# First weights' upper copies and lower parts a tile ahead of use, the first block dealt out anew, U laid out three times

## The chip, the core and the metric

One core of a Trainium2 chip runs the whole program in one launch. The metric is device time in microseconds from start to end of an execution. Engines are named as in the profile: PE (matmul), PEld (its weight loads), DVE, ACT, POOL, and SP, whose queue issues the DMAs.

## The reference

Batch 8, 8 heads, 576 positions, 64 per head, so x is 8 blocks of 576 x 512. All in fp32.

```python
ret = (scale * q @ k.T * Dmat) @ v             # retention, Dmat lower triangular
x   = ret laid out as (B, S, 512)
h   = x.transpose(0, 2, 1) @ U @ V             # U 576 x 32, V 32 x 576: rank 32 over positions
u   = x + h.transpose(0, 2, 1)
x   = u + np.maximum(u @ w_ch1, 0) @ w_ch2     # 512 -> 2048 -> 512
k   = np.maximum(xk @ w_k, 0); v = (k * k) @ w_v
out = sigmoid(xr @ w_r) * v                    # xk, xr: mixes of x and x shifted by one
```

The weights, U and V come in as 64-bit floats, and the kernel makes fp32 of them on the chip.

## The kernel before, in words

An fp32 product is made of three fp32r products: each operand is split into an upper copy (a cast to fp32r by ACT) and a lower part (what the cast left, by DVE or POOL), and upper x upper, lower x upper, upper x lower are summed in PSUM.

The first phase is what the change touches. `seq` runs over 8 batches of 5 chunk pairs (step i is batch i // 5, pair i % 5). A step computes, on PE, `inter(i)` (L842), `own(i)` (L864), `scores(i + 1)` (L808) and `gain(i + 1)` (L886); on DVE `decay`, `from_state`, `states` and `leave`, which end in the tile xt. A step later `natural` transposes xt (PE L950, copied by ACT L960 to xs), two steps later `low_rank` multiplies by U (PE L971, tile gall). When a batch's five are through, its low-rank sum is split (gt), and eight `mix` (PE L1009, DVE L1013) multiply by V and add into xt, which gives u.

Between these the hidden layer of the block of 512 columns before runs: 16 products h (PE L356, `hidden_part`, three parts of four matmuls each), each left by ACT as hs (L362) and stored to DRAM (L367). `FIRST` gives how many h go into each step of the first eight, `FULL` those of the later ones. Half of a step's h come before `stages(2 * i)`, half before `stages(2 * i + 1)`.

The weight w_ch1 is used first by these h. It is cut in four groups of 512 columns (w_0 to w_3; h f uses group f // 4), and each group in four tiles: column half c (h f uses c = (f % 4) // 2), row half j. A tile goes through stages: `load` (SP, L113), `down` (two ACT passes, ca at L97 and cf at L101), `fill` (DVE join L104), and `split` (ACT upper copy w_h L153, DVE lower part w_l L154). The table of `place(...)` says after which half step each stage is written into the program; all engines then run their queues in the written order. `fetch_in_turn` lets only `AHEAD[0]` bytes of loads be under way at once.

Batch 0 is `first_batch()`: no hidden work is there yet, the loads have just begun, and each step runs through its chain alone. `WARM` matmuls on zeros stand ahead of it. After its low-rank sum (`first_sum`) and mixes, h 0 and h 1 are taken together. From step 5 on `step_of(i)` does the above.

Of the kernel before, what the change touches and what calls it, by code (L numbers as in the profile page):

```python
# [9 lines left out]
F32 = mybir.dt.float32  # L10
# [23 lines left out]
WARM = 12  # L34
# [6 lines left out]
def retention_mixer_kernel(ctx: ExitStack, tc: tile.TileContext, io):  # L41
# [67 lines left out]
    AHEAD = [3 << 19]  # L109
# [21 lines left out]
    def convert(fetch, parts, p, n, after=None, eng=nc.gpsimd, halves=False, own=False):  # L131
# [16 lines left out]

        def split():
            h, l = parts()  # L150
            f = got["f"].rearrange("p (k n) -> p k n", n=256) if halves else got["f"]
# [587 lines left out]
    with ExitStack() as st:  # L739
# [223 lines left out]
        gall = []  # L963

        def low_rank(b, p):
            n = CH[p][1]
            if not gall:
                gall.append(bank("g", "gall"))
            x = xn.pop((b, p))
            for k in range(KD):  # L970
                nc.tensor.matmul(  # L971
                    gall[0][32 * k:32 * k + 32, 128 * (b % 4):128 * (b % 4) + 128],
                    ust[:n, p * RANK:(p + 1) * RANK],
                    x[:n, k * 128:(k + 1) * 128],
                    start=(p == 0 and b % 4 == 0),
                    stop=(p == NC - 1),
                    skip_group_check=True,
                )
# [3 lines left out]
        def first_sum(k):  # L982
            if not k:
                gst[0] = a2.tile([96, DM], F32R, tag="gt", name="gt0")
            o, g = slice(k * 128, (k + 1) * 128), gall[0][32 * k:32 * k + 32, 0:128]
            hi, lo, again = (gst[0][r:r + 32, o] for r in (0, 32, 64))
            nc.scalar.copy(hi, g)
            nc.vector.tensor_tensor(lo, g, hi.bitcast(F32), op=ALU.subtract)
            nc.gpsimd.tensor_copy(again, hi.bitcast(F32))

        def low_rank_sum(b):
            gs = small(F32, "gs")[:32]
            gt = a2.tile([96, DM], F32R, tag="gt", name=f"gt{b}")
            for k in range(KD):
                nc.scalar.copy(
                    gs[:, k * 128:(k + 1) * 128],
                    gall[0][32 * k:32 * k + 32, 128 * (b % 4):128 * (b % 4) + 128],
# [52 lines left out]

        def prep_u():
            def fetch():
                raw = big.tile([128, NC * RANK], I64, tag="unit", name="uraw")
# [3 lines left out]
            waiting.append(convert(fetch, lambda: (ust, None), 128, NC * RANK))  # L1057
# [59 lines left out]
        place("u", 1, 2)  # L1117
# [5 lines left out]
        for at in (  # L1123
# [38 lines left out]
        AHEAD[0] = 1 << 20  # L1162
# [3 lines left out]
        load_to(NC + 2)  # L1166
        AHEAD[0] = 0

        def first_batch():
# [6 lines left out]
            for i in range(NC):  # L1176
# [16 lines left out]
                leave(i)  # L1193
                if i:
                    natural(0, i - 1)
                stages(i)
# [6 lines left out]
                if i == 3:  # L1203
                    stages("j0")
# [30 lines left out]
            gain(NC)  # L1235
            decay(NC)
            states(NC)
            ready.extend((0, f) for f in range(2, NF))
# [3 lines left out]
            stages("c1")  # L1242
# [11 lines left out]
        FIRST, FULL = (2, 1, 2, 2, 2, 2, 2, 1), (3, 3, 4, 4, 2)  # L1254
# [349 lines left out]
def _factors(u, v):  # L1604
    u = np.concatenate([u, np.zeros((NC * C - S, RANK), u.dtype)]).reshape(NC, C, RANK)
    return {
        "moe_U": u.transpose(1, 0, 2).reshape(C, NC * RANK),
# [27 lines left out]
```

## Time and profile before

| | us |
|---|---|
| median of 3 runs | 1389.57 (1386.78 to 1391.11) |
| the profiled execution, its own time | 1388.58 |
| its span, first to last instruction | 1386.8 |
| PE busy in the span | 1344.8 (97%) |
| PE's share of the chain that ended last | 89% |
| ACT, DVE, POOL busy | 653.4, 847.7, 338.9 |
| DMA, mean over the span | 222 GB/s |

The page cuts the span into 40 equal slices of 34.7 us and gives the busy share of each engine in each; the phase that the change touches is the first four or five slices. Views of the trace then give busy time by stretch, the waits by who ended them, and the instructions in order of time.

### The profile page before, as it was taken

The page shows a single profiled execution, that of the slowest core. Times are in us where ns is not written, and L with a number is a line of the kernel's source. Part 1 is how long each engine was busy: PE and PEld are TensorE (multiplying, and loading weights), DVE is VectorE, ACT ScalarE, POOL GpSimd, SP SyncE. Part 2 cuts the span into 40 slices and gives each one's busy share as a digit, 9 for nine tenths or more (in the row PEclk, how much of TensorE's full clock was granted, in tenths as well). Part 3 has the DMA queues.
Part 4 walks back from the last instruction along what each step waited for, and adds up shares of the span by engine and source line. Part 5 has one row for each costly group of instructions (what it writes and reads, how often), then busy time and mean ns, then how long its engine had stood idle before and what let it go on. Part 6 is the DMA issues. An engine that isn't in the chain of part 4 may idle for free.

```text
span 1386.8 us, 25835 instructions
## 1 busy us (share of the span) xinstructions
PE 1344.8 (97%) x10296; PEld 1101.0 (79%) x10296; DVE 847.7 (61%) x1175; ACT 653.4 (47%) x1135; POOL 338.9 (24%) x287
## 2 busy tenths in 40 slices
PE   6778899999999999999999999999999999999998
PEld 4556688888888788888887888888888888888897
DVE  3544342333323212689889898698687787787753
ACT  4443344443433455644454444465565455465431
POOL 1111133242131134222122222203303303303312
PEclk8899999999999999999999999999999999999999
DMA  7773669877664465978879696788066075074272
GB/s 247 242 264 123 218 222 322 307 263 256 241 239 156 164 216 201 306 263 280 282 233 334 217 308 217 277 280 318 0 249 237 1 282 203 30 275 151 79 300 77
DMA packets 124377, 307.93 MB, mean 222 GB/s; under 512 B 14496, under 2 KB 27168, under 8 KB 124256
## 3 DMA queue, kind: packets, MB, share of 16 engines
q1 hardware_dynamic: 124256, 306.28, 63.7%
q8 instruction: 81, 1.33, 0.4%
q14 instruction: 40, 0.33, 0.1%
HBM read 215.00 MB, written 91.23 MB: 221 GB/s over the span
## 4 chain that ended last, share of the span: by engine, by line
PE 89%; DVE 2%; ACT 1%; issue 1%; DMA 0%; SPq 0%; DVEq 0%; ACTq 0%
PE h L356 27%; PE v L1471 14%; PE gc L528 6%; PE ga L528 6%; PE gd L528 6%; PE kd L1375 4%; PE kc L1375 4%; PE ka L1375 4%; PE gb L528 3%; PE kb L1375 2%; PE rd L1375 2%; PE rc L1375 2%; PE ra L1375 2%; PE xn L950 1%; PE up L842 1%; PE c L610 1%
## 5 line engine op out<-in xcount | busy, mean ns | idle before, releaser
L362 ACT ACTIVATE hs<-h 128x512 f32<-128x512 f32 x144 | 86.0, 598 | 230.3 <-PE h L356 222.5
L1427 POOL TENSOR_TENSOR vl<-m,vh 128x512 fp32r<-128x512 f32 (+1 forms) x40 | 47.6, 1192 | 310.2 <-ACT vh L1426 240.2
L822 DVE TENSOR_TENSOR pm<-up,dtab 128x512 f32<-128x512 f32 (+1 forms) x40 | 25.5, 637 | 157.2 <-PE up L808 146.3
L487 ACT CAST sbh<-rb 128x1024 fp32r<-128x1024 f32 x64 | 67.3, 1052 | 58.0 <-PE gd L528 47.1
L488 DVE TENSOR_TENSOR sbl<-rb,sbh 128x1024 fp32r<-128x1024 f32 x64 | 85.3, 1333 | 7.9 <-ACT sbh L487 7.7
L1471 PE MATMUL v<-vh,wv_0u 128*128 128x512 f32 x288 | 88.7, 389 | 0.0
L1471 PE MATMUL v<-vh,wv_1u 128*128 128x512 f32 x288 | 88.7, 389 | 0.0
L770 POOL TENSOR_TENSOR kv<-kv,ktab 128x512 f32<-128x512 f32 (+1 forms) x40 | 39.8, 994 | 170.5 <-DMA kv<-in_kv 119.9
L488 DVE TENSOR_TENSOR sal<-ra,sah 128x1024 fp32r<-128x1024 f32 (+1 forms) x64 | 65.5, 1023 | 21.0 <-PE gd L528 13.1
L487 ACT CAST sah<-ra 128x1024 fp32r<-128x1024 f32 (+1 forms) x64 | 53.6, 837 | 50.7 <-DVE ra L469 24.4
L1427 POOL TENSOR_TENSOR vl<-c,vh 128x512 fp32r<-128x512 f32 (+1 forms) x40 | 62.2, 1574 | 25.9 <-ACT vh L1426 25.9
L1471 PEld LDWEIGHTS v<-vh,wv_1u 128*128 128x128 f32 x288 | 54.1, 188 | 11.2
L1471 PEld LDWEIGHTS v<-vh,wv_0u 128*128 128x128 f32 x288 | 53.9, 188 | 11.0
L1426 ACT CAST vh<-m 128x512 fp32r<-128x512 f32 (+1 forms) x40 | 23.2, 579 | 75.3 <-DVE m L1425 75.3
L1013 DVE TENSOR_TENSOR xt<-mx,xt 128x256 f32<-128x256 f32 x64 | 28.9, 457 | 48.6 <-PE mx L1009 48.3
L1471 PE MATMUL v<-vl,wv_0u 128*128 128x512 f32 x144 | 56.0, 389 | 0.0
L1471 PE MATMUL v<-vl,wv_1u 128*128 128x512 f32 x144 | 56.0, 389 | 0.0
L641 ACT ACTIVATE tp<-x2l,omu 128x511 f32<-128x511 f32 x72 | 51.0, 714 | 3.5 <-issue 2.7
L572 POOL TENSOR_TENSOR x<-x,ur 128x512 f32<-128x512 f32 x16 | 24.9, 1572 | 107.7 <-DVE x L568 76.8
L356 PE MATMUL h<-uh,w_0h 128*128 128x512 f32 x144 | 42.9, 421 | 4.0 <-ACT w_0h L153 3.2
L1425 DVE SCALAR_TENSOR_TENSOR m<-m 128x512 f32<-128x512 f32 (+1 forms) x40 | 44.8, 1120 | 1.4
L356 PE MATMUL h<-uh,w_3h 128*128 128x512 f32 x144 | 40.8, 403 | 5.0 <-ACT w_3h L153 5.0
(288 smaller groups left out, 3731.6 us busy)
## 6 DMA issues: line engine op xcount, KB each, us to landing
wk<-keys SPq DMA_DIRECT2D x80, 512.0 KB, 5.9
hp<-hs SPq DMA_DIRECT2D x128, 256.0 KB, 2.7
rb<-hp SPq DMA_DIRECT2D x64, 512.0 KB, 5.9
wr<-gates SPq DMA_DIRECT2D x40, 512.0 KB, 7.4
qk<-in_qk SPq DMA_DIRECT2D x32, 512.0 KB, 5.4
kv<-in_kv SPq DMA_DIRECT2D x32, 512.0 KB, 6.1
ra<-hp SPq DMA_DIRECT2D x32, 512.0 KB, 7.0
ur<-ub SPq DMA_DIRECT2D x18, 512.0 KB, 5.7
```

The source lines that it names most:

```text
L356: nc.tensor.matmul(hps[t, f], w.part(lo, k, fo), u[k // 2][:, k % 2, :], start=(part == 0 and k == 0), stop=(part == 2 and k == KD - 1),)
L362: nc.scalar.activation(h, hps.pop((t, f)), AF.Relu)
L487: nc.scalar.copy(hi_, src)
L488: nc.vector.tensor_tensor(lo_, src, hi_.bitcast(F32), op=ALU.subtract)
L528: nc.tensor.matmul(group[g][p], l[:, col(p)], r, start=(h == 0 and j == 0 and i == 0), stop=(i == 2 and last), skip_group_check=True,)
L641: nc.scalar.activation(tp[:, 1:], x[:, :BT - 1], AF.Copy, scale=omu[:, j, k:k + 1])
L770: nc.gpsimd.tensor_tensor(k, k, ktab[:, p, :n].to_broadcast([128, n, NP, D]), op=ALU.mult)
L1013: nc.vector.tensor_tensor(u, ps[:, :n], u, op=ALU.add)
L1375: nc.tensor.matmul(ps[b], l, r[:, i], start=(part == 0 and i == 0 and j == 0), stop=(i == 1 and j == 2), skip_group_check=True,)
L1425: nc.vector.scalar_tensor_tensor(x, x, 0.0, x, op0=ALU.max, op1=ALU.mult)
L1427: eng.tensor_tensor(l, x, h.bitcast(F32), op=ALU.subtract)
L1471: nc.tensor.matmul(vacc[t][o], w.part(lo, g, col(o)), x[:, i, :], start=(g == 0 and i == 0 and j == 0), stop=(g == NG - 1 and i == 1 and j ...
```

## The change

It does these things, all in the first phase:

- `split` is parted into `upper` (ACT) and `lower` (DVE), each with a place of its own, and the table of places is written anew: a tile's join and upper copy are written one or more half steps ahead of the h that first uses it, and two more tiles (w_1's second column half) are loaded ahead of the hidden work, with a further pair of qk and kv.
- `FIRST` goes from (2, 1, 2, 2, 2, 2, 2, 1) to (2, 1, 2, 1, 1, 2, 2, 3).
- U comes in three times side by side (480 in place of 160 columns). In batch 0 one matmul a chunk, with 96 columns of U stationary and 512 columns of x moving, gives the sum on three groups of 32 partitions; a copy on POOL (`keep`) makes the old `ust` for the later batches. The join of U stands in step 1 in place of step 2.
- The first low-rank sum is split in two halves of 256 columns (one ACT cast of 96 partitions and one DVE subtraction each) in place of four quarters with three instructions each.
- `WARM` is 9 in place of 12, and the loads may be 2 MB ahead at the start (1.5 before) and 1.5 MB at the weights (1 before).

```diff
-WARM = 12
+WARM = 9
-    AHEAD = [3 << 19]
+    AHEAD = [1 << 21]
...
+        def upper():
+            h, l = parts()
+            nc.scalar.copy(h, got["f"].rearrange("p (k n) -> p k n", n=256))
+
+        def lower():
+            h, l = parts()
+            f = got["f"].rearrange("p (k n) -> p k n", n=256)
+            eng.tensor_tensor(l, f, h.bitcast(F32), op=ALU.subtract)
+
+        if halves:
+            return [load, down, fill, upper, lower]
...
         def low_rank(b, p):
-            n = CH[p][1]
-            if not gall:
-                gall.append(bank("g", "gall"))
+            n, c = CH[p][1], p * RANK
             x = xn.pop((b, p))
+            if b == 0:
+                if not p:
+                    gall[0] = bank("g", "g0")
+                nc.tensor.matmul(
+                    gall[0][:96], u_all["x"][:n, 3 * c:3 * c + 96], x[:n], start=(p == 0), stop=(p == NC - 1)
+                )
+                return
...
-        def first_sum(k):
-            if not k:
+        def first_sum(j):
+            if not j:
                 gst[0] = a2.tile([96, DM], F32R, tag="gt", name="gt0")
-            o, g = slice(k * 128, (k + 1) * 128), gall[0][32 * k:32 * k + 32, 0:128]
-            hi, lo, again = (gst[0][r:r + 32, o] for r in (0, 32, 64))
-            nc.scalar.copy(hi, g)
-            nc.vector.tensor_tensor(lo, g, hi.bitcast(F32), op=ALU.subtract)
-            nc.gpsimd.tensor_copy(again, hi.bitcast(F32))
+            gt, g = (x[:96, j * 256:j * 256 + 256] for x in (gst[0], gall[0]))
+            nc.scalar.copy(gt, g)
+            nc.vector.tensor_tensor(gt[32:64], g[32:64], gt[32:64].bitcast(F32), op=ALU.subtract)
...
-            ("w0", "j0", "w joins", "h"), ("w0", "j1", "w joins", "h"), ("w0", "c1", "c1", "c1"), ("w0", "c1", "c1", "c1"),
-            ("w1", 10, 10, 11), ("w1", 10, 11, 11), (10, 12, 13, 14), (10, 13, 14, 14),
-            (11, 14, 15, 16), (11, 15, 16, 16), (13, 16, 17, 18), (13, 17, 18, 18),
-            (15, 18, 19, 20), (15, 19, 20, 20), (17, 20, 21, 22), (17, 21, 22, 22),
+            ("w0", 3, "w joins", "h", "l"), ("w0", "j1", "w joins", "h", "l"),
+            ("w0", "c1", "c1 joins", "c1 h", "c1 h"), ("w0", "c1", "c1 joins", "c1 h", "c1 h"),
+            ("w1", "e", 10, 10, 10), ("w1", "e", 10, 10, 11), ("w2", 11, 12, 13, 13), ("w2", 12, 12, 13, 13),
+            (10, 13, 14, 15, 15), (10, 14, 15, 16, 16), (12, 15, 16, 17, 17), (12, 16, 17, 18, 18),
+            (14, 17, 18, 19, 19), (14, 18, 19, 20, 20), (16, 19, 20, 21, 21), (16, 20, 21, 22, 22),
...
-        AHEAD[0] = 1 << 20
+        AHEAD[0] = 3 << 19
         stages("w0")
         load_to(NC + 1)
         stages("w1")
         load_to(NC + 2)
+        stages("w2")
+        load_to(NC + 3)
         AHEAD[0] = 0
...
             first_sum(0)
+            first_sum(1)
+            stages("h")
             for k in range(KD):
-                if k + 1 < KD:
-                    first_sum(k + 1)
-                if k == KD - 1:
-                    stages("h")
                 for x in range(2):
                     mix(0, k, x)
                 if k % 2:
                     nc.scalar.copy(uh[k // 2], u[:, k - 1:k + 1, :BT])
+            stages("l")
+            stages("c1")
...
-        FIRST, FULL = (2, 1, 2, 2, 2, 2, 2, 1), (3, 3, 4, 4, 2)
+        FIRST, FULL = (2, 1, 2, 1, 1, 2, 2, 3), (3, 3, 4, 4, 2)
```

What the table of places moves is not seen in it, so three places of the order follow.

**ACT at the first tiles of w_3** (w_3h is their upper copies, hs_n leaves h_n, ca and cf are the down passes, xs and xt belong to batches' transposes and sums). Before:

```order
L362 ACTIVATE hs_10_1412<-h_10_1399 128x512
L97 ACTIVATE ca<-w_3_raw_1182 128x512
L101 ACTIVATE cf<-w_3_raw_1182 128x512
L939 COPY xt_1493<-dn_1436 128x4x64
L960 COPY xs_4_1505<-xn_4_1500 64x512
L362 ACTIVATE hs_11_1520<-h_11_1507 128x512
L153 CAST w_3h_1415<-cf 128x2x256
L153 CAST w_3h_1525<-cf 128x2x256
L97 ACTIVATE ca<-w_3_raw_1295 128x512
L101 ACTIVATE cf<-w_3_raw_1295 128x512
L362 ACTIVATE hs_12_1547<-h_12_1534 128x512
```

and with the change:

```order
L972 COPY xs_3_1337<-xn_3_1332 128x512
L374 ACTIVATE hs_8_1352<-h_8_1339 128x512
L151 CAST w_2h_1160<-cf 128x2x256
L97 ACTIVATE ca<-w_3_raw_1140 128x512
L101 ACTIVATE cf<-w_3_raw_1140 128x512
L151 CAST w_3h_1357<-cf 128x2x256
L97 ACTIVATE ca<-w_3_raw_1253 128x512
L101 ACTIVATE cf<-w_3_raw_1253 128x512
L951 COPY xt_1444<-dn_1387 128x4x64
L972 COPY xs_4_1456<-xn_4_1451 64x512
L374 ACTIVATE hs_9_1471<-h_9_1458 128x512
L151 CAST w_3h_1366<-cf 128x2x256
```

h_12 is the first to use w_3. Its two upper copies stood between hs_11 and hs_12; they now stand behind hs_8 and hs_9, three and two h ahead.

**PE at the end of batch 1's low-rank sum** (mx are its eight mixes, h_15 is the last h of block 0). Before:

```order
L1009 MATMUL mx_1_0_1805<-vst,gt_1640 128x256
L842 MATMUL up_1813<-qk_3_1422,w_5_1632 64x64 x8
L842 MATMUL up_1813<-qk_3_1422,w_6_1767 64x64 x8
L864 MATMUL dn_1830<-pm_1763,kv_3_1424 64x64 x16
L808 MATMUL up_1813<-qk_4_1555 64x64 x8
L971 MATMUL gall<-xs_1_1781,ust 32x128 x4
L950 MATMUL xn_2_1864<-ident,xt_1493 128x128 x4
L1009 MATMUL mx_1_1_1871<-vst,gt_1640 128x320
L1009 MATMUL mx_2_0_1874<-vst,gt_1640 128x256
L1009 MATMUL mx_2_1_1877<-vst,gt_1640 128x320
L1009 MATMUL mx_3_0_1880<-vst,gt_1640 128x256
L1009 MATMUL mx_3_1_1883<-vst,gt_1640 128x320
```

and with the change:

```order
L1027 MATMUL mx_1_0_1747<-vst,gt_1585 128x256
L368 MATMUL h_14_1750<-uh_0_631,w_3h_1357 128x512 x2
L368 MATMUL h_14_1750<-uh_1_632,w_3h_1366 128x512 x2
L1027 MATMUL mx_1_1_1755<-vst,gt_1585 128x320
L368 MATMUL h_14_1750<-uh_0_631,w_3l_1358 128x512 x2
L368 MATMUL h_14_1750<-uh_1_632,w_3l_1367 128x512 x2
L1027 MATMUL mx_2_0_1762<-vst,gt_1585 128x256
L368 MATMUL h_14_1750<-ul_0_633,w_3h_1357 128x512 x2
L368 MATMUL h_14_1750<-ul_1_634,w_3h_1366 128x512 x2
L1027 MATMUL mx_2_1_1772<-vst,gt_1585 128x320
L368 MATMUL h_15_1775<-uh_0_631,w_3h_1357 128x512 x2
L368 MATMUL h_15_1775<-uh_1_632,w_3h_1366 128x512 x2
```

Five mixes in a row with nothing between them are now parted by four matmuls of h each; the last two of the eight stand in h_15 in the same way.

**DVE in batch 0 at the join of U** (xt is written by leave, pm by decay, y by from_state). Before:

```order
L822 TENSOR_TENSOR pm_481<-up_415,dtab 128x512
L923 TENSOR_TENSOR y_483<-up_415,qtab 128x512
L911 TENSOR_TENSOR w_6_485<-dn_448,w_5_396 128x256
L911 TENSOR_TENSOR w_7_487<-dn_448,w_6_485 128x256
L940 TENSOR_TENSOR xt_312<-dn_448,y_483 128x4x128
L104 SCALAR_TENSOR_TENSOR ust<-ca,cf 128x160
```

and with the change:

```order
L952 TENSOR_TENSOR xt_314<-dn_359,y_394 128x4x128
L104 SCALAR_TENSOR_TENSOR u_405<-ca,cf 128x480
L834 TENSOR_TENSOR pm_486<-up_420,dtab 128x512
L935 TENSOR_TENSOR y_488<-up_420,qtab 128x512
L923 TENSOR_TENSOR w_6_490<-dn_453,w_5_398 128x256
L923 TENSOR_TENSOR w_7_492<-dn_453,w_6_490 128x256
L952 TENSOR_TENSOR xt_314<-dn_453,y_488 128x4x128
```

The join of U, three times as wide, stood behind the five instructions of a step and now stands ahead of them.

## Rows read from the trace of the kernel before

**Rows 1.** The page, 40 slices of 34.7 us: PE busy tenths, PE's granted clock.

```profile
PE   6778899999999999999999999999999999999998
...
PEclk8899999999999999999999999999999999999999
```

**Rows 2.** Busy time by stretch (us from start): PE, PEld, DVE, ACT, POOL, PEclk, DMA share, GB/s.

```profile
0.00:53.20 53.20, 38.76 (x824) 27.50 (x824) 22.77 (x47) 21.30 (x50) 9.76 (x17) 0.81 0.68 217
53.20:130.00 76.80, 60.07 (x892) 44.63 (x892) 35.55 (x62) 36.91 (x69) 10.22 (x9) 0.93 0.64 224
130.00:152.00 22.00, 18.37 (x275) 13.62 (x274) 10.69 (x20) 5.46 (x9) 2.08 (x2) 0.84 0.52 183
152.00:300.00 148.00, 147.86 (x2080) 120.65 (x2080) 51.11 (x96) 68.45 (x130) 46.38 (x44) 1.00 0.80 274
300.00:1387.00 1087.00, 1079.69 (x6230) 894.60 (x6228) 727.56 (x951) 521.31 (x877) 270.50 (x216) 1.00 0.62 216
...
43.60:53.20 9.60, 9.54 (x136) 7.31 (x136) 3.14 (x5) 3.66 (x6) 1.04 (x1) 0.78 0.27 97
```

**Rows 3.** Who PE waited for, 53.2 to 152 us: total us, times, longest.

```profile
PE h L356 <- ACT w_3h L153: 5.0, 4, 1.4
PE h L356 <- ACT w_2h L153: 4.9, 4, 1.3
PE h L356 <- ACT w_1h L153: 3.4, 3, 1.2
PE h L356 <- ACT w_0h L153: 3.2, 2, 1.8
PE mx L1009 <- DVE xt L1013: 2.2, 4, 0.6
```

**Rows 4.** The same for PE, 0 to 53.2 us.

```profile
PE dn L886 <- POOL kv L770: 3.4, 3, 2.1
PE gall L971 <- DVE ust L104: 2.4, 1, 2.4
PE mx L1009 <- POOL gt L989: 2.3, 2, 1.5
```

**Rows 5.** ACT and DVE in order of time at w_3 (start, duration, idle before).

```profile
111.43 0.60 ACT L362 ACTIVATE hs<-h 128x512 f32<-128x512 f32 x1 [1.36 <-PE h L356]
111.93 0.61 ACT L153 CAST w_3h<-cf 128x512 fp32r<-128x512 f32 x1
...
114.01 0.62 ACT L153 CAST w_3h<-cf 128x512 fp32r<-128x512 f32 x1 [1.47 <-DVE cf L104]
114.53 0.67 ACT L97 ACTIVATE ca<-w_raw 128x512 f32<-128x512 f32 x1
...
113.23 0.68 DVE L104 SCALAR_TENSOR_TENSOR cf<-ca,cf 128x512 uint32<-128x512 uint32 x1
```

**Rows 6.** PE in order of time within one step of batch 1.

```profile
83.78 0.43 PE L971 MATMUL gall<-xs,ust 128*32 128x128 f32 x8
84.14 0.66 PE L950 MATMUL xn<-ident,xt 128*128 128x128 f32 x4
84.55 1.18 PE L356 MATMUL h<-uh,w_1h 128*128 128x512 f32 x4
85.57 1.08 PE L356 MATMUL h<-uh,w_1l 128*128 128x512 f32 x4
```

**Rows 7.** ACT and DVE from the first low-rank sum to the last mix addition.

```profile
35.55 0.26 ACT L987 CAST gt<-gall 32x128 fp32r<-32x128 f32 x1 [0.54 <-PE gall L971]
36.16 0.26 ACT L987 CAST gt<-gall 32x128 fp32r<-32x128 f32 x1 [0.35 <-DVE gt L988]
...
36.76 0.82 DVE L1013 TENSOR_TENSOR xt<-mx,xt 128x256 f32<-128x256 f32 x2
...
42.64 0.81 DVE L1013 TENSOR_TENSOR xt<-mx,xt 128x256 f32<-128x256 f32 x2
```

**Rows 8.** Who SP's queue waited for, 50 to 150 us.

```profile
SPq L367 <- ACT hs L362: 66.3, 16, 8.8
```

More of the change, by code (lines that the diff above doesn't have):

```diff
@@ L147, in fill @@
             join(f if l is not None else h, got["a"], f.bitcast(U32))
+        def upper():
[7 more added lines that the diff above has]
+            return [load, down, fill, upper, lower]
         def split():
             h, l = parts()
-            f = got["f"].rearrange("p (k n) -> p k n", n=256) if halves else got["f"]
+            f = got["f"]
             if l is not None:
@@ L960, in natural @@
             nc.scalar.copy(xn[b, p][:n], ps[:n])
-        gall = []
+        gall = {}
         def low_rank(b, p):
-            n = CH[p][1]
-            if not gall:
-                gall.append(bank("g", "gall"))
+            n, c = CH[p][1], p * RANK
             x = xn.pop((b, p))
+            if b == 0:
[5 more added lines that the diff above has]
+                return
+            new = p == 0 and b in (1, 4)
+            if new:
+                gall[1] = bank("g", f"g{b}")
             for k in range(KD):
                 nc.tensor.matmul(
-                    gall[0][32 * k:32 * k + 32, 128 * (b % 4):128 * (b % 4) + 128],
-                    ust[:n, p * RANK:(p + 1) * RANK],
+                    gall[1][32 * k:32 * k + 32, 128 * (b % 4):128 * (b % 4) + 128],
+                    ust[:n, c:c + RANK],
                     x[:n, k * 128:(k + 1) * 128],
-                    start=(p == 0 and b % 4 == 0),
+                    start=new,
                     stop=(p == NC - 1),
@@ L1049, in hidden, with parts, keep @@
                         slot()
+        u_all = {}
         def prep_u():
             def fetch():
-                raw = big.tile([128, NC * RANK], I64, tag="unit", name="uraw")
+                raw = big.tile([128, NC * 3 * RANK], I64, tag="unit", name="uraw")
                 fetch_in_turn(raw, io["moe_U"])
                 return raw
-            waiting.append(convert(fetch, lambda: (ust, None), 128, NC * RANK))
+            def parts():
+                if "x" not in u_all:
+                    u_all["x"] = small(F32, "u3")[:, :NC * 3 * RANK]
+                return u_all["x"], None
+            def keep():
+                nc.gpsimd.tensor_copy(
+                    ust.rearrange("p (c r) -> p c r", r=RANK),
+                    u_all["x"].rearrange("p (c r) -> p c r", r=3 * RANK)[:, :, :RANK],
+                )
+            waiting.append(convert(fetch, parts, 128, NC * 3 * RANK)[:3] + [keep])
         def prep_v():
@@ L1116, in retention_mixer_kernel @@
         prep_u()
-        place("u", 1, 2)
+        place("u", 1, "u join", "u join")
         prep_v()
@@ L1193, in first_batch @@
                 leave(i)
+                stages(i)
+                if i == 1:
+                    stages("u join")
                 if i:
                     natural(0, i - 1)
-                stages(i)
                 if i > 1:
@@ L1235, in first_batch @@
             gain(NC)
+            stages("c1 joins")
             decay(NC)
             states(NC)
+            stages("c1 h")
             ready.extend((0, f) for f in range(2, NF))
@@ L1241, in first_batch @@
                     hidden_part(0, f, part)
-            stages("c1")
+            stages("e")
             split_u(1, 0, u[:, :, BT:], S - BT)
```

9 lines of the change are left out of this document (4 added, 5 removed).

## The prediction

> **What bounds the kernel now.** I read the page's slices first. PE is busy 9 tenths in all but the first five slices, and its clock is clearly below the top level only in the first two [rows 1]; so the kernel is bound by PE, and the only time to be had lies in the first 170 us. Cut by what the program does there [rows 2], the span has five parts: batch 0 alone (0 to 53.2 us) with PE busy 38.8; block 0's hidden work with its weight conversion (53.2 to 130), PE busy 60.1 of 76.8; the rest of it (130 to 152), 18.4 of 22; a stretch of 148 with PE busy 147.9; and 1087 with 7.3 us idle. The last two are not touched: every instruction after block 0 keeps its place on its engine, and merely starts earlier. So what counts is 14.4 us of idle PE in batch 0, 16.7 in the second part and 3.6 in the third, and the lower clock there.
>
> Who PE waited for [rows 3]: from 53.2 to 152 us, the matmuls that first use a weight tile waited for ACT's upper copy of it, 5.0 + 4.9 + 3.4 + 3.2 = 16.5 us in 13 waits. That is nearly all the idle time of the second part. The mixes' waits for DVE's additions, 2.2 us, are most of the third part's.
>
> Why ACT is late is seen in its order of time [rows 5]: hs ends the last product at 111.43, only then comes the first upper copy, the second waits 1.47 us for a join that DVE does at 113.23 behind a lower part that itself waited for the first copy. ACT is not short of time: 36.9 busy of 76.8 [rows 2]. The copy merely stands behind the h before it.
>
> In batch 0 PE waited 2.4 us for U (ust), 2.3 for the split of the low-rank sum (gt) and 3.4 for scaled kv [rows 4].
>
> **The change part by part.**
>
> *Upper copies ahead, minus 16.5.* Nothing is added; five stages stand where four stood. By the order shown, each copy stands at least one h ahead of its use, three parts of some 1.0 us each [rows 6]. I walked ACT and DVE through steps 5 to 11 with the durations of [rows 5]: hs 0.60, upper copy 0.61, down passes 0.67 and 0.65, join 0.68. A pair of tiles costs ACT 2 x (0.61 + 0.67 + 0.65) = 3.9 us and DVE 2 x (0.68 + 0.69) = 2.7, the lower part priced like a join. All 13 waits go. What is late next is DVE's own chain: in steps 6, 8 and 9, which have only one h, the step's `leave` and `from_state` now stand behind two joins and two lower parts. My walk leaves PE waiting about 0.5 us for `leave` in step 7 and 0.8 in step 10; I take 1.5 for such waits, between 0 and 4.
>
> *FIRST: the last step gets three h, minus 3.6.* All eight mixes stand between parts of h (1.0 us each), longer than the 0.41 of an addition [rows 7]. The four waits of 0.6 go, and with them the other 1.4 us of the third part, which are one wait for xs and one for uh that follow the bare mixes.
>
> *Clock, minus 7.1.* With PE busy 60.1 at a mean granted clock of 0.93 and 18.4 at 0.84 [rows 2], the lower level cost 60.1 x 0.07 + 18.4 x 0.16 = 4.2 + 2.9 = 7.1 us. The next part, where PE idles 0.1 us, has 1.00. If PE stays busy I expect 1.00 here too. Bounds: 0 and 7.1.
>
> *U three times, minus 2.0.* The join of U moves ahead of a step's five DVE instructions, into time in which DVE waits for PE; at 480 columns it takes at most the 0.68 of 512. The wait of 2.4 goes. Against it stand five longer products. Now four products of 32 columns stand side by side and the next work starts 0.36 us later; 512 columns of transposes take 0.41 in one pass [rows 6], and an fp32 product has two records per instruction, so 0.82 for the new one, 0.46 more. Four of the five lie in PE's idle time in batch 0; the last is on the path: 2.4 - 0.46 = 2.0. Bounds: an equal cost (2.4) and a wait for ACT, which now has 2 x 0.65 more for U, of about 1 us (1.4).
> The Trainium skill, "TensorEngine Tiling (Array Packing)", section "Theoretical Speedup", speaks against this part: a product with 32 stationary columns gains up to four times by standing beside three others, which the change gives up. By that, 4 x 0.36 = 1.44 us, and the gain here would be 1.3 in place of 2.0; no run here shows it yet.
> The bytes grow by 320 KB, at 217 to 274 GB/s [rows 2] 1.2 to 1.5 us of loading before kv of the fourth pair; more loads under way and three warm matmuls fewer give about as much back, since the start waits for loads. I take 0, between +1.5 and -1.
>
> *First sum in halves, minus 2.9.* From the first gt (35.55) to the end of the last mix addition (42.64 + 0.81 = 43.45) it takes 7.9 us now [rows 7]: four rounds of ACT, DVE, POOL, 0.61 apart, with an upper copy of u and two of weights between the third and fourth. Now there are two rounds, ACT then DVE, of about 0.8 us (nearest rows: 0.26 for a quarter of the columns, 0.41 for an addition of 256), then eight additions in a row, 4 x 0.82 = 3.3: 5.0 in all. Bounds: 1.9 and 3.5.
>
> *Clock of the first h, minus 1.0.* From 43.6 to 53.2 PE is busy 9.54 at 0.78 [rows 2], which costs 2.1 us. The idle time ahead is shorter, not gone, so I take half; bounds 0 and 2.1. The second column half of w_0 is converted under it; that its copies come in time is in the first term.
>
> Sum: -16.5 - 0.2 (small waits of the second part) - 3.6 - 7.1 + 1.5 - 2.0 - 2.9 - 1.0 = -31.8. The profiled execution took 1388.6 (span 1386.8), so about **1357**. The median of the runs shown is 1.0 above that execution, well inside the 0.3% (4 us) that a measurement of this kernel can tell from no change.
>
> **The rivals.**
>
> *Conversion stays the bound in the steps with one h.* In the shortened second part ACT and DVE have 36.9 and 35.6 us of work in about 56, two thirds, and less where a step has one h. If in steps 6, 8 and 9 PE waits as now, twice 1.2 us, and the clock falls as often, 7.2 + 4 of the gain go back: 1368. For it: strict queues, and my walk has margins under 1 us there. Against it: the tiles are a half step or more ahead.
>
> *Loads become the bound.* The two parts move 76.8 x 224 + 22 x 183 = 21.2 MB; in some 70 us that is 300 GB/s, more than the 274 that ran under a fully busy PE at a DMA share of 0.80 [rows 2]. At 274 they need 77 us: 7 us lost, 1364. Against it: a share of 1 would be 340, and some 3 MB move ahead of the hidden work.
>
> *Slower than before: a raw tile comes too late.* SP's queue holds the loads behind stores that wait for hs, 66 us in all, up to 8.8 [rows 8]; with one h a step the next load is issued later against its use, and ACT, waiting for a raw tile, would hold up the hs and state copies behind it. There are four such pairs among the hidden work. To eat 32 us each would have to be 8 us late, a whole step; 1393 if 9. The walk has the loads landing 1 to 5 us ahead.
>
> *Batch 0 gives nothing.* If loading sets its pace with U's bytes, the 5.9 us of the last three terms shrink to zero: 1363.
>
> A change that doesn't do what it says I rule out: the order of each engine shows every move.
>
> **How the numbers follow.** My forecast, with all terms inside their bounds: 0.70, 1352 to 1363. Batch 0 gives nothing: inside that at its upper end, 0.08. Conversion stays: 0.14. Loads: 0.06. A late tile, slower: 0.02. The best case is every term at its good bound: no residual waits (1.5), clock of the first h (1.1), U (0.4), first sum (0.6), start (1): 1352; I put the low end a little under it. The range is **1351 to 1368**. All cases but the last are faster by far more than 4 us: faster 0.97, within 0.3% 0.01, slower 0.02.
>
> **What would show it.** Right: no row "h <- ACT w_h" among PE's waits after batch 0; PE at 9 tenths from the second slice on and its clock at the top from about 50 us; the last addition of batch 0's mixes near 38 us; h_0 of block 1 some 32 us earlier than now. Wrong: waits of PE for `leave` or `from_state` of more than 1 us in steps 7 to 10 (then conversion is still the bound); waits of ACT or POOL for DMAs with PE behind them; products of U of over 1 us; a clock that falls although PE is busy.

## The result, and the profile after

| | kernel before | changed kernel |
|---|---|---|
| median | 1389.62 us (1386.78 to 1391.11) | 1349.99 us (1349.82 to 1352.0) |
| the profiled execution, span | 1388.58 us, 1386.8 | 1349.82 us, 1348.0 |

The ratio is 0.972, with a 95% interval of 0.9702 to 0.9738. Forecast were 1357 us and a range of 1351 to 1368: the sign and the place were right, the gain (38.8 us between the two profiled executions, 31.8 forecast) was too small, and the median lies 1 us below the range. Three later measurements of the same changed kernel (below) gave 1351.7 to 1353.9, so the low end of the range is about where the kernel lies; the gain is 36 to 40 us.

The page of the changed kernel: busy time by engine, then the slices of PE and of its granted clock, which answer to [rows 1].

```profile
PE 1332.4 (99%) x10263; PEld 1096.0 (81%) x10263; DVE 845.5 (63%) x1173; ACT 652.1 (48%) x1133; POOL 337.4 (25%) x284
...
PE   7999999999999999999999999999999999999998
...
PEclk8899999999999999999999999999999999999999
```

PE stands at 9 tenths from the second slice on, where it took five slices before. To see where the time went I cut both traces at the same instructions: at the first `inter` of block 0's hidden work (step 5, behind h_0 and h_1), and at the `inter` of step 14, one step behind the eight of the first block. This is called the stretch from here on. In the rows, `up` is what `scores` and `inter` write, `dn` what `own` and `gain` write, `y` what `from_state` writes, and `g` or `gall` the low-rank sum. Busy time by stretch (us from start: length, PE busy, granted clock, DMA share, GB/s), the kernel before:

```profile
51.28:158.28 107.00, 86.58 (x1305) 0.92 0.61 212
```

and the changed kernel:

```profile
45.03:120.53 75.50, 75.07 (x1306) 1.00 0.78 273
```

The same instructions of PE, within one record, take 75.50 us in place of 107.00. So the 38.8 us are 6.25 ahead of this stretch (51.28 to 45.03), 31.5 in it, and 1.05 behind it. Who PE waited for in that stretch of the changed kernel (total us, times, longest):

```profile
PE up L854 <- DVE y L935: 0.3, 1, 0.3
```

This one row stands where [rows 3] stood: in this execution no wait for an upper copy is left, none for a mix's addition, and the clock is at its upper level, 2.4 GHz, throughout.

Ahead of the stretch, DVE, ACT and PE in order of time (start, duration, and in brackets idle time before and who ended it); these answer to [rows 7], the last two to the first `h`:

```profile
19.69 0.94 DVE L104 SCALAR_TENSOR_TENSOR u<-ca,cf 128x480 uint32<-128x480 uint32 x1
...
31.98 0.37 ACT L1006 CAST gt<-g 96x256 fp32r<-96x256 f32 x1 [1.19 <-PE g L983]
...
32.83 0.37 ACT L1006 CAST gt<-g 96x256 fp32r<-96x256 f32 x1 [0.48 <-DVE gt L1007]
...
33.68 3.20 DVE L1031 TENSOR_TENSOR xt<-mx,xt 128x256 f32<-128x256 f32 x8
...
38.20 3.25 PE L368 MATMUL h<-uh,w_0h 128*128 128x512 f32 x8
...
45.03 0.46 PE L854 MATMUL up<-qk,w 64*64 64x64 f32 x16
```

The first gt starts at 31.98 where it was 35.55 (3.6 us earlier); from there to the end of the last addition it is 4.9 us (36.88) where it was 7.9; from there to step 5 it is 8.15 us where it was 7.83 (51.28 less 43.45). Who PE waited for up to step 5, which answers to [rows 4]:

```profile
PE dn L898 <- POOL kv L782: 3.1, 3, 1.5
...
PE mx L1027 <- DVE gt L1007: 1.0, 1, 1.0
...
PE g L983 <- ACT xs L972: 0.8, 1, 0.8
PE mx L1027 <- DVE xt L1031: 0.6, 1, 0.6
```

The waits for U and for POOL's gt are gone; the one for scaled kv has stayed.

### The profile page after: what moved, and what is told of

Its sections match the earlier page's. It is cut to its first block, busy times and chain, and to the rows that moved or that the text cites. A ratio compares the mean times of both kernels' runs of the same rounds, so it can differ in the third digit from the quotient of the medians.

```text
span 1348.0 us, 25775 instructions
## 1 busy us (share of the span) xinstructions
PE 1332.4 (99%) x10263; PEld 1096.0 (81%) x10263; DVE 845.5 (63%) x1173; ACT 652.1 (48%) x1133; POOL 337.4 (25%) x284
## 4 chain that ended last, share of the span: by engine, by line
PE 93%; DVE 4%; DMA 1%; issue 1%; ACT 1%; SPq 0%; POOL 0%; DVEq 0%; ACTq 0%
PE h L368 29%; PE v L1507 14%; PE ga L540 6%; PE gc L540 6%; PE gd L540 5%; PE kc L1411 4%; PE kd L1411 4%; PE ka L1411 4%; PE gb L540 3%; PE kb L1411 2%; PE rd L1411 2%; PE rc L1411 2%; PE ra L1411 2%; PE xn L962 2%; PE up L854 1%; PE dn L876 1%
## 5 line engine op out<-in xcount | busy, mean ns | idle before, releaser
L557 POOL TENSOR_TENSOR m<-m,ur 128x512 f32<-128x512 f32 x8 | 12.2, 1557 | 133.6 <-ACT m L554 133.6
L1411 PE MATMUL kc<-kht,wk 128*128 128x512 f32 (+1 forms) x160 | 45.5, 368 | 0.0
```

The source lines that it names most:

```text
L1411: nc.tensor.matmul(ps[b], l, r[:, i], start=(part == 0 and i == 0 and j == 0), stop=(i == 1 and j == 2), skip_group_check=True,)
```

## The experiments

Of the stretch's 31.5 us the prediction's terms give 25.9 (16.5 + 0.2 + 3.6 + 7.1 - 1.5). Two explanations of the missing 5.6 us were set against each other. Theory A: a wait costs its idle time in the profile, and the clock is apart from it. Theory B: a stop of PE costs more than its idle time. A third question was which part of the change carries the gain. "The changed kernel" and "the kernel before" are meant wherever a diff starts from them.

**Which edit on the first weights.** First, the changed kernel with the old FIRST (ratio to the kernel before 0.9797, 0.978 to 0.9815; 1362.2 us).

```diff
-        FIRST, FULL = (2, 1, 2, 1, 1, 2, 2, 3), (3, 3, 4, 4, 2)
+        FIRST, FULL = (2, 1, 2, 2, 2, 2, 2, 1), (3, 3, 4, 4, 2)
```

> The changed kernel with the old table FIRST alone: the first block deals its tiles out 2, 1, 2, 2, 2, 2, 2, 1 as before, upper copies and lower parts stay ahead of their use. Changed kernel 1350.0 us, kernel before 1389.6. Theory A (the price of a wait of TensorE is its idle time in the profile, and the clock is apart from it): the conversion of the first layer's tiles has one upper copy of 1.2 to 1.4 us still exposed in front of the first of each pair in four steps, 5 us of idle time, the mixes that stood bare in front of those steps come back (3.6 us), and 2 to 4 us of clock: 1361 us. Theory B (a stop costs its idle time, some 0.16 us at its head and 0.28 us for two matmuls that stand between two stops): 1363 to 1364. Theory C (FIRST does nothing once the copies are ahead): 1350 to 1352, and no wait for an upper copy between 53 and 130 us.

PE's waits in its stretch (total us, times, longest):

```profile
PE mx L1027 <- DVE xt L1031: 2.2, 4, 0.6
PE h L368 <- ACT w_2h L151: 1.5, 2, 0.8
PE h L368 <- ACT w_3h L151: 1.5, 2, 0.7
```

Theory C falls: four single copies and the bare mixes are back, as A and B both said, though the copies' waits are 0.7 to 0.8 us and not 1.2. The time is 8 to 12 us over the changed kernel's and lies between what A and B forecast, so it doesn't tell these two apart. One such stop tells more, PE in order of time, beside the same groups without a stop:

```profile
64.96 1.07 PE L368 MATMUL h<-uh,w_1h 128*128 128x512 f32 x4
65.87 1.07 PE L368 MATMUL h<-uh,w_1l 128*128 128x512 f32 x4
...
72.72 0.61 PE L368 MATMUL h<-uh,w_2h 128*128 128x512 f32 x2
74.14 0.73 PE L368 MATMUL h<-uh,w_2h 128*128 128x512 f32 x2 [0.80 <-ACT w_2h L151]
74.71 0.62 PE L368 MATMUL h<-uh,w_2l 128*128 128x512 f32 x2
```

A whole group of four starts 0.91 us ahead of the next (64.96 to 65.87). The stopped one starts 1.99 ahead of it (72.72 to 74.71): 1.08 us lost, where 0.80 is shown as idle. The rows' durations overlap in a stream and don't at a stop, which hides 0.28 us in busy time. The kernel before shows the same in the stretch itself. Its step 6 has one stop for an upper copy, of 1.00 us:

```profile
63.91:70.52 6.61, 5.61 (x145) 1.00 0.98 324
```

It takes 6.61 us at the full clock, and the same 145 matmuls take 5.36 in the changed kernel (52.49 to 57.85): 1.25 us lost, 0.25 of them in no idle row.

Next, the changed kernel with the old table of places (loads and joins where they were, copy and lower part right ahead of their tile): ratio 0.9829 (0.9811 to 0.9847), 1365.9 us.

```diff
-            ("w0", 3, "w joins", "h", "l"), ("w0", "j1", "w joins", "h", "l"),
-            ("w0", "c1", "c1 joins", "c1 h", "c1 h"), ("w0", "c1", "c1 joins", "c1 h", "c1 h"),
-            ("w1", "e", 10, 10, 10), ("w1", "e", 10, 10, 11), ("w2", 11, 12, 13, 13), ("w2", 12, 12, 13, 13),
...
+            ("w0", "j0", "w joins", "h", "h"), ("w0", "j1", "w joins", "h", "h"),
+            ("w0", "e", "e", "e", "e"), ("w0", "e", "e", "e", "e"),
+            ("w1", 10, 10, 11, 11), ("w1", 10, 11, 11, 11), (10, 12, 13, 14, 14), (10, 13, 14, 14, 14),
...
```

> The changed kernel with the old places of the first weights alone: the upper copy and the lower part stand in one stage right ahead of their tile again, loads and joins at the old stages; FIRST, U and the low-rank sum as changed. Changed kernel 1350.0 us, kernel before 1389.6. If the early copies carry the gain (as the prediction has it: 16.5 us for them): 13 waits for an upper copy are back between 50 and 130 us, and the time is 1366 or more. If the dealing of FIRST carries it, since h_8, h_10, h_12 and h_14 now stand behind a step's border: only the waits for w_0 and w_1 return, some 6 us, with 2 us of clock: about 1358. Theory B on top of either: 0.4 us for every pair of waits.

It came out at the time of the one case with the rows of the other: only w_0's and w_1's copies wait again (3.2 and 2.4 us), not thirteen, but its stretch is 85.95 us with 8 us not busy at a clock of 0.98, and it starts at 50.06 us. Then the two edits alone, on the kernel before. FIRST alone: ratio 0.9849 (0.9831 to 0.9866), 1368.8 us.

```diff
-        FIRST, FULL = (2, 1, 2, 2, 2, 2, 2, 1), (3, 3, 4, 4, 2)
+        FIRST, FULL = (2, 1, 2, 1, 1, 2, 2, 3), (3, 3, 4, 4, 2)
```

> The kernel before with the new FIRST alone (2, 1, 2, 1, 1, 2, 2, 3). Kernel before 1389.6 us. If FIRST carries the gain: the waits for w_2h and w_3h (9.9 us of idle time), the bare mixes (3.6) and some of the clock (3 to 5) go: 1371 to 1374. If it needs the early copies: the waits only move to other steps, 1383 to 1389. Theory B adds some 2 us to whatever idle time goes.

```profile
PE h L356 <- ACT w_1h L153: 3.4, 3, 1.2
PE h L356 <- ACT w_0h L153: 3.2, 2, 1.8
...
PE h L356 <- ACT w_2h L153: 0.3, 1, 0.3
```

The time is below both of its cases. These waits of PE (45 to 160 us) show why: the new dealing by itself takes away all but 0.3 of the 9.9 us for w_2 and w_3, since their first h now stand behind a step's border, and the old late copy is in time there.

The places alone: ratio 0.9865 (0.9848 to 0.9882), 1370.6 us.

```diff
+        if halves:
+            return [load, down, fill, upper, lower]
...
+        stages("w2")
+        load_to(NC + 3)
...
```

> The kernel before with the upper copies and lower parts set a tile ahead alone (their new places, and the third pair's load with them), old FIRST, old U and old sum. Kernel before 1389.6 us. If the early copies carry the gain alone: the waits for an upper copy go (16.5 us by their idle time, 20 by theory B) and the clock rises, the bare mixes stay: 1366 to 1370. If half of the copies stay exposed without FIRST (two tiles to convert in a step of two h): 1374 to 1380. Together with the run of the new FIRST alone it tells whether the two edits add up or stand for each other: gains that add to the 31 us between h_2 and the end of the first block, or a sum well above or below it.

The time lies between its two cases: the waits for w_0 and w_1 are gone, those for w_2 and w_3 are 1.5 each and the mixes are bare. Both edits together (the two diffs above), with nothing else of the change: ratio 0.9805 (0.9791 to 0.9818), 1363.7 us.

> The kernel before with both edits on the first weights, FIRST and the places, and nothing else of the change: U once, the sum in quarters, the old allowance, 12 warm products. Kernel before 1390 us; FIRST alone gave 21.2 us and the places alone 19.4. If the two do not stand for each other: 40 us, 1350. By the stretch of the two traces from h_2 to the step behind the first block (31.4 us): 1357 to 1359. If each takes most of what the other takes: 1365.

Neither of the clean cases: 26.8 us, where the single gains add to 40.6. Its stretch is 81.82 us (49.95 to 131.77), 6.3 longer than the changed kernel's, and PE's waits in it say why:

```profile
PE dn L898 <- issue: 2.3, 1, 2.3
PE up L854 <- DVE y L935: 1.2, 1, 1.2
PE dn L898 <- POOL kv L782: 0.7, 1, 0.7
```

None is for weights. 0.7 us is for a kv that comes late. The 2.3 us stand inside a `dn`, and this row doesn't tell what ended them; a stop of 2.0 to 2.3 us stands inside that `dn` in all three runs that have the early copies and the old sum, and in none with the new sum. It isn't the sum's, though: with the new sum the same count of matmuls falls on a row of h, and four executions stop there, up to 2.3 us (the last section has what PE waited for). So the loads and the sum are left to be tried.

**The allowance.** The changed kernel with the old one: ratio 0.9784 (0.9764 to 0.9803), 1359.5 us.

```diff
-    AHEAD = [1 << 21]
+    AHEAD = [3 << 19]
...
-        AHEAD[0] = 3 << 19
+        AHEAD[0] = 1 << 20
```

> The changed kernel with the old allowance of bytes in flight, 1.5 MB for U and V and 1 MB behind them, in place of 2 and 1.5 MB. Changed kernel 1350.0 us. The prediction gave the loads nothing (between 1.5 us of loss and 1 of gain). If the earlier first tiles come from it (GpSimd's first kv at 9.16 us in place of 10.43): 1351 to 1352. If the place of the loads in SP's queue decides and not the allowance: 1350, and the first kv stays near 9.2 us.

It missed by 6 us or more: beside the changed kernel's ratios (0.972 to 0.9729) the allowance is worth about 8. SP's and POOL's rows in order of time, with the old allowance:

```profile
46.60 2.21 SPq L113 DMA_DIRECT2D w_raw<-in_moe_w_ch  x2
...
53.09 0.34 SPq L113 DMA_DIRECT2D kv<-in_kv  x1
...
58.98 1.19 POOL L782 TENSOR_TENSOR kv<-kv,ktab 128x512 f32<-128x512 f32 x1 [9.46 <-DMA kv<-in_kv]
```

and the same transfers in the changed kernel:

```profile
37.18 1.63 SPq L113 DMA_DIRECT2D w_raw<-in_moe_w_ch  x2
...
41.85 0.34 SPq L113 DMA_DIRECT2D kv<-in_kv  x1
...
46.64 1.04 POOL L782 TENSOR_TENSOR kv<-kv,ktab 128x512 f32<-128x512 f32 x1 [5.38 <-DMA kv<-in_kv]
```

That kv is issued 11 us later. PE then waits 2.6 us for it, in one stop, and the step lasts 9.78 us where it lasts 5.36 in the changed kernel. The wait's other 1.8 us are in the rows behind it:

```profile
60.23 0.69 PE L898 MATMUL dn<-kv 64*64 64x64 f32 x32 [2.59 <-POOL kv L782]
...
61.58 2.06 PE L368 MATMUL h<-uh,w_1h 128*128 128x512 f32 x4
63.43 1.51 PE L368 MATMUL h<-uh,w_1l 128*128 128x512 f32 x4
```

A group of four starts 1.85 and 1.35 us ahead of the next in place of 0.91: the granted clock is 0.72 of full speed from 60 to 66 us. Two edits on top of it then tried whether the order on SP or the room decides. The tile before the awaited one moved ahead of the weights gave 1360.1 us (ratio 0.9775, 0.9755 to 0.9796):

```diff
-        stages("w1")
         load_to(NC + 2)
+        stages("w1")
         stages("w2")
```

> The changed kernel with the old allowance of bytes in flight, and the load of the third kv tile of block 1 put ahead of the weights' loads in SP's order in place of behind them. The run with the old allowance alone was 1359.5 us, the changed kernel 1350 to 1352.4. If that tile, queued behind the weights (issued at 53.1 us in place of 41.9, TensorE's wait 2.6 us for GpSimd's kv), is what the allowance costs there: the wait goes and 4 us with it, 1355. If the weights, now later, take its place: a wait for an upper copy or a join, and 1358 to 1361.

The wrong tile, for the awaited one was again issued at 53.01 us and waited for 3.3. So the awaited one was moved (1362.3 us, ratio 0.98, 0.9782 to 0.9818):

```diff
         stages("w1")
-        load_to(NC + 2)
+        load_to(NC + 3)
         stages("w2")
-        load_to(NC + 3)
```

> The changed kernel with the old allowance of bytes in flight, and the last of block 1's early kv tiles (the fourth in the listing of GpSimd's kv from 28 us on, or the one before it) loaded ahead of the third pair of weights instead of behind it. The run that moved the tile before it was 1360.1 us, with the old allowance alone 1359.5; in both the awaited tile was issued at 53.0 to 53.1 us, behind the weights. If the awaited tile is this one: it is issued near 47 us, TensorE's wait for kv between 48 and 130 us (2.6 us) goes, and the stretch from the first to the last step of the first block falls from 80.0 to 75.6 us, the time to 1355. If what counts is the room in the allowance and not the order: issued after 51 us again, and 1358 to 1361.

It is issued at 49.58 and its wait is gone (step 6 lasts 5.36 us again). But the pair behind it is late in its place, PE's waits there:

```profile
PE up L820 <- DMA qk<-in_qk: 2.1, 1, 2.1
PE dn L898 <- POOL kv L782: 1.3, 1, 1.3
```

So the order only picks which tile is late; the queue as a whole is. From 23.7 to 53.2 us the run with the old allowance moved 221 GB/s and the changed kernel 299. More still, 4 and 2 MB, brought nothing (1354.7 us, ratio 0.9738, 0.9724 to 0.9752, against 0.9726 for the changed kernel beside it):

> The changed kernel with more bytes in flight, 4 MB for U and V and 2 MB behind them, in place of 2 and 1.5. If the allowance sets when the first tiles land (the run with the old allowance had GpSimd's fourth kv at 22.18 us, the run with one bank 19.87): the fourth kv is 1 to 2 us earlier and the time with it. If more transfers side by side delay each one, as the old allowance suggests it was meant to avoid: the kv tiles later and the time 1 to 4 us longer.

The fourth kv came at 18.47 us against 20.75 in the changed kernel beside it and 19.08 in its first execution, and the time did not follow.

**U and the sum.** The changed kernel with the old U, join and quarters: ratio 0.9785 (0.9766 to 0.9805), 1359.3 us.

```diff
-                nc.tensor.matmul(
-                    gall[0][:96], u_all["x"][:n, 3 * c:3 * c + 96], x[:n], start=(p == 0), stop=(p == NC - 1)
-                )
...
+            nc.gpsimd.tensor_copy(again, hi.bitcast(F32))
...
-        place("u", 1, "u join", "u join")
+        place("u", 1, 2)
```

> The changed kernel with the old U and the old low-rank sum: U laid out once, its join back at its old place, three packed products of 32 columns in place of one of 96 rows for each part, and the first block's sum in quarters with GpSimd's copy. Changed kernel 1350.0 us. The prediction's terms for these two parts are 2.0 and 2.9 us: 1354.9. By the moments in the two traces (first gt 3.6 us earlier, last addition of the first mixes 6.6 us earlier): 1355 to 1357. If the array's packing were worth four times, as one rule has it, the old products would be cheaper than the new ones and the time under 1354.

It is 5 to 9 us over the changed kernel: the prediction's 4.9 is just below that, and the packing's "under 1354" falls. Step 5 starts at 49.85 us against 45.0 to 47.7 in four executions of the changed kernel, about 3.3 later than their mean; and the stretch is 78.96 against 75.5 to 77.7 in the same four, 2.4 above their mean, with the stop of 2.0 us inside a `dn` that was met above and one of 0.8 of the same kind. Only the 3.3 us, known to no better than the scatter of the start, can be put down to U and the sum.

**The price of a stop by itself.** In block 2, where nothing stops PE, all h in one PSUM bank (1363.4 us, ratio 0.9807, 0.9785 to 0.9829):

```diff
-            hps[t, f] = turn("h", (0, 1), f"h{t}_{f}")
+            hps[t, f] = turn("h", (0, 1) if t != 2 else (0,), f"h{t}_{f}")
```

> The changed kernel with one edit in a late block, where nothing stops TensorE and the clock is full: all 16 h of block 2 share one PSUM bank instead of two in turn, so that each waits for the copy out of the one before. That makes up to 15 stops of the same kind, between one h's last group and the next one's first. Changed kernel 1350.0 us. Theory A (a stop costs the idle time that the profile shows in front of it): the time grows by just the sum of those idle times. Theory B (a stop costs more than its idle time, about 0.16 us at its head): by that sum and 2 to 3 us. The stretch between the same two instructions in the two traces tells it free of the runs' scatter. If the clock falls there, both come with its loss on top, which the granted clock of the stretch tells.

The stretch between the same two `inter`, its length, PE busy and clock, and PE's waits in it:

```profile
170.90:239.85 68.95, 61.66 (x806) 1.00 0.77 267
...
PE h L368 <- ACT hs L374: 7.3, 11, 0.7
```

The same stretch in the changed kernel:

```profile
166.17:224.65 58.48, 58.48 (x806) 1.00 0.88 309
```

It is 10.47 us longer, with 7.3 us of idle time in 11 stops and the clock at 1.00 in both: 3.2 us, 0.29 for a stop, are in no idle row. Theory A falls. A second run doubled the copy that PE waits for (1372.8 us, ratio 0.9871, 0.9846 to 0.9895):

```diff
-            nc.scalar.activation(h, hps.pop((t, f)), AF.Relu)
+            ps = hps.pop((t, f))
+            for again in range(2 if t == 2 else 1):
+                nc.scalar.activation(h, ps, AF.Relu)
```

> The run with one bank in block 2, where ScalarE copies each of that block's h out twice (the second copy writes the same values), so that each stop is some 0.6 us longer. In the run with one bank 11 stops of 0.69 us idle (7.3 in all) made the stretch between the same two steps 10.47 us longer: 0.29 us above the idle time per stop, at the full clock. If the excess is a fixed price of a stop: idle 1.3 us each, excess again 0.25 to 0.32 us per stop. If it is a share of the wait (0.29 of 0.69): 0.5 to 0.55 us per stop. If longer waits let the clock fall, the granted clock of the stretch is under 1.00 and the excess is larger by that.

```profile
171.03:246.94 75.91, 61.71 (x805) 1.00 0.69 243
...
PE h L368 <- ACT hs L376: 14.2, 11, 1.3
```

It is 17.43 us longer, 14.2 of it idle: again 3.2 us over 11 stops, 0.29 each. So between waits of 0.69 and 1.3 us it is a fixed price of a stop and no share of the wait.

**The clock of the first h.** One product on zeros behind each of batch 0's mixes (1355.0 us, ratio 0.975, 0.9731 to 0.9768):

```diff
                     mix(0, k, x)
+                    nc.tensor.matmul(
+                        spare, warm[:, 0, :], warm.to_broadcast([128, 4, 128]), start=True, stop=True
+                    )
```

> The changed kernel with eight more products on zeros (128 x 512, two-byte, nothing reads them), one behind each mix of the first batch, where the first h of the block start at the low clock. Changed kernel 1350.0 us. If the fill between the mixes raises the clock before the first h: h_0 and h_1 take 5.5 us instead of 8.2 from the last addition on, and the gain is 2 us, less what the products cost: 1348. If the products only stand in the way of the mixes (0.2 to 0.4 us each, where VectorE's additions pace them): 1350 to 1353 with the clock as before.

PE's busy time and clock in this run:

```profile
35.00:36.00 1.00, 1.00 (x5) 0.50 0.92 277
...
39.00:40.00 1.00, 1.00 (x3) 0.50 0.84 322
...
41.00:42.00 1.00, 1.00 (x42) 1.00 0.91 317
```

The first h stand at the upper level (7.0 us from the last addition to step 5, 8.15 in the changed kernel), but the products are slow at the lower one, and from the first mix to the last addition it now takes 6.3 us (33.89 to 40.20) where it took 3.9, which eats it; the time is 2 us above the slower of the two cases. Then seven products in the two waits ahead of the mixes alone (1355.8 us, ratio 0.9747, 0.9722 to 0.9773):

```diff
             low_rank(0, NC - 2)
+            fill(3)
             low_rank(0, NC - 1)
+            fill(4)
```

> The changed kernel with seven products on zeros that nothing reads, three in TensorE's wait for the last xs and four in its wait for the first gt, none between the mixes. If these two waits (0.82 and 1.00 us at 30 to 33 us) are what the clock falls after at 34.0: it stays at its upper level through the first scores and h, and the time from the first mix to the first step of block 1 falls from 12.0 to 9.5 us, the total by 2 to 2.5. If the mixes themselves, which VectorE's additions pace, let it fall: no change, or up to 0.3 us slower.

```profile
37.00:38.00 1.00, 1.00 (x23) 1.00 0.97 344
38.00:39.00 1.00, 1.00 (x56) 0.52 0.96 346
...
40.00:41.00 1.00, 1.00 (x4) 0.50 0.93 330
41.00:42.00 1.00, 1.00 (x4) 0.77 0.95 289
```

The fall comes at 38.0 us in place of 33.9 and lasts 3.4 us in place of 6.8, so the waits move it and don't make it alone: 11.0 us from the first mix to step 5 in place of 12.1. The median shows nothing of it, and can't be held against it: behind step 5 this execution has 5.0 us of stops of the kind that the last section takes up, and a second fall of the clock (65.4 to 68.8 us). 12 warm products in place of 9 changed nothing that can be told either (1354.6 us, ratio 0.9739, 0.9724 to 0.9753):

```diff
-WARM = 9
+WARM = 12
```

> The changed kernel with 12 warm products in place of 9. The prediction gave this edit nothing. If it costs nothing: the time of the changed kernel in the same round, within 1.5 us. If nine leave the clock too low at the start: up to 2 us faster; if three more of them stand in front of the first scores: up to 1 us slower.

**The mark.** The changed kernel itself, unedited, beside these runs: 1352.4 us (ratio 0.9726, 0.9712 to 0.9739), 1351.7 (0.9722, 0.9701 to 0.9743) and 1353.9 (0.9729, 0.971 to 0.9749).

> The changed kernel itself once more, as the mark for the other runs, since in the run with one bank the first instructions, which are the same, stand 3.8 us later (the first mix at 36.75 us against 32.94). If the start of the program differs from chip to chip: the first mix near 36 us and 1353 to 1355 us. If it was that run's own: near 33 us and 1350.

> The changed kernel once more, as the mark for the run with the filled waits: 1350 to 1353 us.

> The changed kernel once more, as the mark for the run with the moved kv tile: 1350 to 1353 us.

The first mix stands at 34.62, 35.94 and 34.30 us in them: the start scatters by some 3 us from execution to execution, so steps ahead of 45 us are known to no better than that. No run was faster than the changed kernel.

## Why the prediction fell short, and where it was right

*Upper copies ahead* and *FIRST*: the idle time went as the steps said. 20.3 us of waits in the stretch became 0.3 in the profiled pair, so the gross terms of 16.5, 0.2 and 3.6 hold. What the prediction put down to the copies alone, the runs divide otherwise: FIRST by itself removes the 9.6 us of w_2 and w_3, the early copies are needed for w_0 and w_1, and either edit alone gives half or more.

*Residual waits of 1.5 for `leave` and `from_state`*: 0.3 in two of the four executions of the changed kernel, 1.2 in the other two, at the head of step 10 (the third, 0 to 130 us):

```profile
PE up L854 <- ACT w_2h L151: 1.2, 1, 1.2
```

The row names an upper copy, but `inter` doesn't read one. In the third execution it starts 0.14 us behind the end of `from_state`'s y, as it does in the first (0.15), and a join of DVE ahead of y took 1.53 us there in place of 0.69. So the place was forecast rightly (0.8 in step 10); against the profiled pair the term was too large by 1.2.

*The price of a wait* is the step that failed. "Upper copies ahead, minus 16.5" took the idle column as the cost. With 0.29 us for each of the 13 stops, which the run with one bank measured at the full clock, they cost 3.8 us more. 25.9 + 1.2 + 3.8 = 30.9 of the 31.5 measured. The account closes no better than to some 1.5 us: at the same price the other seven stops of the stretch (mixes, xs, uh, `leave`) would cost 2.0 more, where 0.6 is left; against that, the changed kernel's step 7 takes 9.09 us where its step 11, with the same work, takes 8.44, with no idle row to tell of it. The clock's 7.1 stands within that remainder; no run measured it alone.

*U three times*: the first gt came 3.6 us earlier in the profiled pair, not 2.0; the difference is within the start's scatter. The product's price of 0.82 was near: in the run with one bank, whose start is the changed kernel's, it takes 0.86 to the next work.

```profile
31.51 1.02 PE L983 MATMUL g<-xs,u 128*96 128x512 f32 x2
32.37 0.60 PE L962 MATMUL xn<-ident,xt 128*64 128x128 f32 x4
```

Against the 0.36 us of the four packed products that is 2.4 times. The Trainium skill, "TensorEngine Tiling (Array Packing)", section "Theoretical Speedup", gives up to four times for 32 columns. The 2.4 lies inside that; four times, which would have made the product 1.44 us, did not come here.

*First sum in halves*: 4.9 us against 5.0 forecast and 7.9 before. *Clock of the first h, minus 1.0*: wrong, +0.3; the clock fell at 33.9 us, with the mixes, though the wait ahead was shorter. The three terms of batch 0 together were 5.9 forecast and 6.25 measured in the profiled pair. That they agree so well is luck in part: against the same execution of the kernel before, the other three of the changed kernel, which reach step 5 at 46.56 to 47.71 us, give 3.6 to 4.7.

*The loads, 0* was right for this change and for the wrong reason. The term weighed U's bytes against "more loads under way" and did not see that the allowance had to grow for the other terms to come true: at the old one, shorter steps meet kv tiles that are late, and 8 us go back. That is the rival "loads become the bound", 7 us by its own working from bytes and rate, and the mechanism is the one it named in its price, but it was the room in flight that set the rate. At the new allowance the stretch ran at 273 GB/s and nothing in it waited for a load.

Of the other rivals, conversion as the bound had no row in the profiled execution, and in two others the 1.2 us at step 10; a raw tile too late had none. Behind the stretch 0.6 us less is waited for sal, a lower part of a later layer; the rest of the 1.05 us there is not explained.

## What to carry to other kernels

A wait of TensorE costs more than the idle time beside it (here by 0.25 to 0.29 us): measure from the start of the group in front to the start of the one behind, and compare with the same pair in a stream. When a change removes many stops from a stretch, ask what its transfers will be late for at the new pace, and read the rate that the allowance of bytes in flight lets through, not only the bytes. Two edits that each remove "the" wait can stand for each other; try them alone and together before dividing a gain among them.

## What was not expected of the hardware

The price of a stop did not depend on its length: 0.29 us at 0.69 and at 1.3 us of idle time, with the clock at 1.00.

The clock stood at its lower level for up to five microseconds in which PE was busy 1.00, both in the run with a product behind each mix (35 to 40 us) and at 38 to 41 us in the one with filled waits. PE being busy now did not give it back at once.

Executions of one program differ in short stops of PE that the profile puts down to "issue". In the third execution of the changed kernel two of them stand among the h, one of 0.78 us at 66.34, and the page's queue of instructions has one transfer that ends 1.4 us ahead of that (63.8 to 65 us):

```profile
PE h L368 <- issue: 1.5, 2, 0.8
...
q8 instruction: 1, 0.02, 6.1%
```

The first execution of it has neither; its stretch is 75.50 us, this one's 77.74. What these stops are can be read from all the traces together. Counting PE's matmuls from the start, 39 of them stand at the numbers 221, 348, 474, 980, 1107, 1487 and 1614 (or one further), which lie whole numbers of some 127 apart, whatever instruction falls there: number 1107 is a `dn` with the old sum (2.0 to 2.3 us) and a row of h with the new one (0.8 to 2.3). All 39 end 1.2 to 1.7 us behind the end of a transfer on the queue that the page lists as instruction; of PE's 333 other waits later than 10 us from the start, 3% do. So at these places PE waits, by these rows, for its own next instructions, 0.2 to 4.6 us at a time. What makes them come late in one execution and in time in another no run tells, and 17 other stops put down to issue, 16 of them of 1.2 us at matmul 185 or 188, are not of this kind.
